# First four token tiles transposed on TensorE, all weight and cache loads moved to one DMA queue, and the MLP's place in the schedule shifted

## The chip, the cores and the metric

The kernel runs on one core of a Trainium2 chip. The core has TensorE (PE, matrix products into PSUM), VectorE (DVE), ScalarE (ACT), GpSimd (POOL) and SyncE (SP, which here only issues DMAs), and 16 DMA engines that move data between HBM and the on-chip memory (SBUF). DMAs can be issued from the queues of SP, ACT and POOL. Each engine runs its own instructions in order and waits for others by semaphores. The metric is the device time of one launch in microseconds, lower is better.

## The reference

The input `x` has 2048 tokens of 512 channels. It is layer-normalised once; the result goes through an attention block against a cache of 32 heads with 2048 keys each, and through an MLP whose first half shifts four quarters of its channels by one or two tokens. The two results are combined with `x`.

```python
xn = layernorm(x)                                  # 2048 x 512
q = (xn @ wq) as 32 heads of 128
p = softmax(q @ k_cache^T * 128 ** -0.5)           # per head 2048 x 2048
s = concat_heads(p @ v_cache) @ wo                 # 2048 x 512
h = gelu(xn @ w1)                                  # 2048 x 512
hs = token_shift(h by +1, -1, +2, -2 per quarter) @ w2
x1 = xn + hs
g = silu(x1 + gelu(layernorm(x1) @ w3) @ w4)       # w3: 512 x 1792, w4: 1792 x 512
return x + s * g
```

All data are bfloat16 in HBM; products accumulate in float32.

## The kernel before

**Tiling.** Tokens are cut into 16 tiles of 128 (NT) and 4 query blocks of 512 (QT). Heads come in 8 groups of four (HG, NG). One *unit* is one head against one query block of 512 tokens; there are 128 units, ordered by group, then query block, then head (line 113). A unit has 8 *slots* (SPU); in each slot TensorE makes the scores of 256 keys (`s_slot`, two 128x512 products into PSUM tile `ps_s`) and ScalarE turns them into exponentials `pT` (line 168). The product with V (`pv_slot`, tile `ps_o`) follows five slots later (LAG).

**What else a slot carries** is decided by hand in the loop of lines 516 to 576, by the slot number p within the unit. Slots 0 and 1: the query product of the next unit (`q_mm`, PSUM tag "xa", one buffer). Slot 0: the last additions for the softmax sum of the unit before (`add_last`, three DVE instructions). Slot 2: DVE copies the query out of PSUM (`q_copy`, line 155), and scales the output of the unit before the last (`norm`, line 218). Slot 3: `sums` (four small products, again PSUM tag "xa", then a reciprocal, then a DMA of it to HBM, line 206). Slot 4: `bcast`, the DMA that reads it back to all partitions (tile `rb`, line 210). Slots 4 and 5: the output projection of one finished token tile (`wo_mm`, also tag "xa"), read out by DVE in slot 6 (`wo_post`). Slots 2, 3 and 6, 7: half a *chunk* of the MLP each.

**The MLP.** 136 chunks are spread evenly over *windows* of half a unit, from window W0 to W1 (lines 488 and 566). First come 16 chunks of xn @ w1 (`m1_chunk`), then 16 chunks of the shifted product with w2 (`m2_chunk`), each followed by `x1` (one DVE instruction that reads PSUM tile `ps_m`) one slot later and `stats` (two DVE instructions, lines 363 and 364, and two on GpSimd) two slots later, then alternating w3 and w4 chunks. Work that belongs some slots later is put down with `at(n, fn)` and runs at the end of slot n.

**The layer norm.** `ln1_stats` loads a token tile and takes mean and variance on DVE; `rsqrt` makes 1/sqrt(var + eps) with two small GpSimd instructions; `ln1_apply` normalises on DVE (line 272), transposes the tile by a DMA on SP's queue into `xnT` (line 275), and stores it to HBM for the MLP (line 276). The first four tiles are done before the loop, the other twelve one per four slots, from slot 1 on (lines 510 to 513).

**Order and queues.** `pin` (line 61) holds an instruction in program order on its engine; what is not pinned a scheduler places. All matmuls, all DVE and ACT compute and all DMAs on SP's queue are pinned; the DMAs and the compute on POOL's queue mostly are not. On SP's queue: loads of K, transposed on the way, in four pieces of 128 KB per head (line 128), the transposes of xn, the two small softmax-sum DMAs of each unit, and the stores of the result. On POOL's queue: V (512 KB per head, line 134), wq (line 139), wo (line 143), w1 and w2 (lines 328, 329), w3 and w4, and the token tiles. The K, V, wq and wo of the next group are loaded during the last query block of a group, one head per unit (lines 520 to 529). Before the loop all four heads of the first group are loaded, and w1, w2 and wo:

```python
    for t in range(4):
        ln1_apply(t)
    for h in range(1, HG):
        load_w(h)
        load_k(h, range(KSPLIT))
        load_v(h)
    ph1_load()
    ...
    q_mm(0, range(DC))
    q_copy(0)
```

Of the kernel before, what the change touches and what calls it, by code (L numbers as in the profile page):

```python
# [17 lines left out]
def kernel(  # L18
# [15 lines left out]
    nc = tc.nc  # L34
# [42 lines left out]
    nc.vector.memset(nhalf[:], -0.5)  # L77

# [4 lines left out]
    qtp = ent(pool("qt", 2))  # L83
# [24 lines left out]
    def rsqrt(out, var):  # L108
        ve = smp.tile([P, 1], FP32, name="ve")
        nc.gpsimd.tensor_scalar(out=ve[:], in0=var, scalar1=EPS, scalar2=None, op0=ALU.add)  # L110
        nc.gpsimd.tensor_tensor(out=out, in0=ve[:], in1=nhalf[:], op=ALU.pow)
# [9 lines left out]


# [9 lines left out]
    def load_v(h):  # L132
        vBs[h] = vp.tile([P, KC, Dh], BF16, name="vb")
        nc.gpsimd.dma_start(  # L134
            out=vBs[h][:], in_=A_v_cache[0, h].rearrange("(kc p) d -> p kc d", p=P))

    def load_w(h):
        wqs[h] = wqp.tile([P, DC, Dh], BF16, name="wq_h")
        nc.gpsimd.dma_start(out=wqs[h][:], in_=wq_v[:, :, h * Dh:(h + 1) * Dh])  # L139

    def load_wo(h):
        wos[h] = wop.tile([P, D], BF16, name="wo_h")
        nc.gpsimd.dma_start(out=wos[h][:], in_=A_wo[h * Dh:(h + 1) * Dh, :])
# [89 lines left out]
    def fin_load(t):  # L233
        xl = tokp.tile([P, D], BF16, tag="ta", name="xl")
        nc.gpsimd.dma_start(out=xl[:], in_=xsrc[t])
        gl = tokp.tile([P, D], BF16, tag="ta", name="gl")
        nc.gpsimd.dma_start(out=gl[:], in_=g_d[t][:])
        fin[t] = (xl, gl)
# [19 lines left out]
    def ln1_stats(t, eng):  # L258
        xin = tokp.tile([P, D], BF16, tag="ta", name="xin")
        eng.dma_start(out=xin[:], in_=xsrc[t])  # L260
        bn = smp.tile([P, nc.vector.BN_STATS_DIM], FP32, name="bn")
        mv = smp.tile([P, nc.vector.BN_AGGR_DIM], FP32, name="mv")
        rs = smp.tile([P, 1], FP32, name="rs")
        pin(nc.vector.bn_stats(out=bn[:], in_=xin[:]))
        pin(nc.vector.bn_aggr(out=mv[:], in_=bn[:]))
        rsqrt(rs[:], mv[:, 1:2])
        ln[t] = (xin, mv, rs)

    def ln1_apply(t):
        xin, mv, rs = ln.pop(t)  # L270
        xn = tokp.tile([P, D], BF16, tag="tb", name="xn")
        pin(nc.vector.tensor_scalar(
            out=xn[:], in0=xin[:], scalar1=mv[:, 0:1], scalar2=rs[:],
            op0=ALU.subtract, op1=ALU.mult))
        pin(nc.sync.dma_start_transpose(out=xnT[:, :, t * P:(t + 1) * P], in_=xn[:]))
        nc.gpsimd.dma_start(out=xn_d[t][:], in_=xn[:])
# [50 lines left out]
    def ph1_load():  # L327
        nc.gpsimd.dma_start(out=w1_sb[:], in_=B_w1.rearrange("(dc p) j -> p dc j", p=P))
        nc.gpsimd.dma_start(out=w2_sb[:], in_=B_w2.rearrange("(jc p) c -> p jc c", p=P))
        for jc in range(DC):  # L330
            b = BASE_J[jc]
            nc.gpsimd.memset(hT[:, jc, 0:b], 0.0)
            nc.gpsimd.memset(hT[:, jc, b + Sq: Sq + PADW], 0.0)
# [9 lines left out]

    def m2_chunk(t):
        def run(i, n):
            if i == 0:
                mlp["ps"] = psX.tile([P, 512], FP32, tag="xm", name="ps_m")
                mlp["xr"] = tokp.tile([P, D], BF16, tag="tb", name="xr")
                nc.gpsimd.dma_start(out=mlp["xr"][:], in_=xn_d[t][:])
# [3 lines left out]
            if i == 1:  # L353
# [13 lines left out]
                at(n + 1, x1)  # L367
                at(n + 2, stats)
# [11 lines left out]
    def ln2(c, n):  # L380
        def start():
            mlp["xn2T"] = mp.tile([P, DC, 512], BF16, name="xn2T")
            xs = []
            for ts in range(4):
                xr = tokp.tile([P, D], BF16, tag="ta", name="x1r")
# [14 lines left out]
        for ts in range(4):  # L400
            at(n + 8 + 2 * ts, lambda ts=ts: apply(ts))
# [22 lines left out]
    def w3_prefetch():  # L424
        if w3_order:
            c, fc = w3_order.popleft()
            w = mp.tile([P, DC, 2 * P], BF16, tag="w3", bufs=3, name="w3_sb")
            nc.gpsimd.dma_start(out=w[:], in_=w3_v[:, :, fc * P:(fc + 2) * P])  # L428
# [4 lines left out]
    def m4_chunk(t, part):  # L433
# [3 lines left out]
        def run(i, n):  # L437
            if part == 0 and i == 0:
                mlp["ps"] = psX.tile([P, 512], FP32, tag="xm", name="ps_m")
                mlp["xr"] = tokp.tile([P, D], BF16, tag="tb", name="xr")  # L440
# [5 lines left out]
            if part == 2 and i == 1:  # L446
# [15 lines left out]
                at(n + 1, x2)  # L462
                at(n + 3, tanh)
                at(n + 5, silu)
# [4 lines left out]
    for tt in range(QT):  # L469
        for jc in range(DC):  # L470
            chunks.append(m1_chunk(tt, jc))
    for t in range(NT):
# [15 lines left out]
    W0, W1 = 4, 2 * (NU - 8)  # L488
# [4 lines left out]
    ln1_engs = [nc.sync, nc.scalar, nc.sync, nc.scalar]  # L493
    for t in range(4):
        ln1_stats(t, ln1_engs[t])
    load_w(0)
    load_k(0, range(KSPLIT))
    load_v(0)
    for t in range(4):
        ln1_apply(t)  # L500
    for h in range(1, HG):
        load_w(h)
        load_k(h, range(KSPLIT))
        load_v(h)
    ph1_load()
    for h in range(HG):
        load_wo(h)
    q_mm(0, range(DC))
    q_copy(0)
    for k, t in enumerate(range(4, NT)):  # L510
        n0 = 1 + 4 * k
        at(n0, lambda t=t: ln1_stats(t, nc.gpsimd))
        at(n0 + 4, lambda t=t: ln1_apply(t))

    wo_todo = deque()
    for n in range(NS + 3 * SPU):
        u, p = divmod(n, SPU)
        if u < NU:
            g, qt, hh = units[u]
            if g + 1 < NG and qt == QT - 1:  # L520
                h = (g + 1) * HG + hh
                if p == 5:
                    load_k(h, (0, 1))
                elif p == 6:
                    load_v(h)
                    load_w(h)
                elif p == 7:
                    load_k(h, (2, 3))
                    load_wo(h)
# [4 lines left out]
        if p in (0, 1) and u + 1 < NU:  # L534
# [3 lines left out]
        if p == 2 and u + 1 < NU:  # L538
# [75 lines left out]
```

## Time and profile before

| | us |
|---|---|
| median of three timed runs | 1324.67 (1320.32 to 1326.06) |
| the profiled execution, its own time | 1323.47 |
| its span, first to last instruction | 1321.7 |
| TensorE busy | 1270.7 (96%) |
| ScalarE busy | 1112.5 (84%) |
| VectorE busy | 1024.5 (78%) |
| GpSimd busy | 220.2 (17%) |
| start of the first matmul | 20.71 |
| start of the first score product | 23.36 |
| first score product of unit 4 | 68.34 |

The table is read as follows. TensorE is the engine with the most work, and a matmul of 512 columns is followed by the next after about 0.215 us at the full clock, though its own record is longer (0.38 us) because matmuls overlap in the array. What TensorE does not spend busy is 51 us. Times in the trace count from the span's start; the profiled execution's own time is 1.8 us longer than its span.

### The profile page before, as it was taken

How to read it: one execution, taken by the hardware profiler on the slowest of the kernel's cores; microseconds unless marked ns; L12 is line 12 of the kernel's file. 1: busy time of each engine (PE TensorE's matmuls, PEld its weight loads, DVE VectorE, ACT ScalarE, POOL GpSimd, SP SyncE). 2: the span in 40 equal slices, each digit the busy share in tenths (PEclk: the TensorE clock that was granted, in tenths of full speed). 3: DMA queues.
4: the chain of work that ended last, by engine and by line, in shares of the span. 5: the costliest groups of instructions: out<-in, count | busy, mean ns of one | idle time of the engine just before them, and what ended most of it. 6: DMA issues, size and time to landing. Idle time of an engine off the chain costs nothing.

```text
span 1321.7 us, 17163 instructions
## 1 busy us (share of the span) xinstructions
PE 1270.7 (96%) x6208; PEld 575.4 (44%) x6208; DVE 1024.5 (78%) x1402; ACT 1112.5 (84%) x1185; POOL 220.2 (17%) x356
## 2 busy tenths in 40 slices
PE   3899999999999999999999999999999999999995
PEld 1344444444444444444444444444444444444442
DVE  1898788888787877788877777888777888777886
ACT  2799988778999988899988889998888999888882
POOL 6630122333211021100111011001010100000101
PEclk9899999999999999999999999999999999999997
DMA  9741373234823267222652127423292312712223
GB/s 217 189 102 27 53 140 84 72 85 112 151 57 70 55 116 124 61 41 44 127 114 60 48 49 121 96 56 65 62 146 57 64 33 48 132 29 52 81 67 88
DMA packets 144468, 112.29 MB, mean 85 GB/s; under 512 B 112320, under 2 KB 114880, under 8 KB 144384
## 3 DMA queue, kind: packets, MB, share of 16 engines
q1 hardware_dynamic: 126496, 57.19, 25.0%
q0 software_dynamic: 17600, 53.76, 15.8%
q8 instruction: 48, 0.79, 0.3%
q14 instruction: 36, 0.29, 0.1%
q10 hardware_dynamic: 288, 0.26, 0.1%
HBM read 81.53 MB, written 8.65 MB: 68 GB/s over the span
## 4 chain that ended last, share of the span: by engine, by line
PE 79%; DVE 9%; ACT 6%; DMA 3%; issue 2%; POOL 1%; DVEq 0%; POOLq 0%; SPq 0%
PE ps_s L106 29%; PE ps_o L106 27%; PE ps_m L106 8%; PE ps_wo L106 8%; PE ps_q L106 6%; ACT pT L168 4%; DVE acc L179 3%; PE ps_sum L106 1%; DVE acc L184 1%; DVE qT L155 1%; ACT sq L286 1%; DMA rb<-dr 1%; DMA xin<-in_A_x_dram 1%; ACT pre L316 1%; DVE gl L250 1%
## 5 line engine op out<-in xcount | busy, mean ns | idle before, releaser
L168 ACT ACTIVATE pT<-ps_s 128x1024 bf16<-128x1024 f32 x1024 | 1015.8, 1029 | 183.0 <-PE ps_s L106 179.0
L106 PE MATMUL ps_s<-qT,kT 128*128 128x512 bf16 x2048 | 611.2, 380 | 5.0 <-DVE qT L155 2.7
L106 PE MATMUL ps_o<-pT,vb 128*128 128x512 bf16 x2048 | 610.0, 380 | 0.0
L179 DVE TENSOR_TENSOR acc<-acc,pT 128x2048 bf16<-128x2048 bf16 x256 | 312.5, 1221 | 75.2 <-ACT pT L168 70.0
L106 PEld LDWEIGHTS <-vb 128*128 128x128 bf16 x2048 | 200.0, 98 | 243.0 <-issue 1.9
L106 PEld LDWEIGHTS <-kT 128*128 128x128 bf16 x2048 | 196.4, 98 | 244.2 <-issue 26.8
L174 DVE TENSOR_TENSOR acc<-pT 128x2048 bf16<-128x2048 bf16 x128 | 156.0, 1219 | 30.9 <-ACT pT L168 30.8
L106 PE MATMUL ps_q<-xnT,wq_h 128*128 128x512 bf16 x512 | 153.9, 383 | 20.7 <-DMA xnT<-xn 20.7
L106 PE MATMUL ps_wo<-wo_h,oT 128*128 128x512 bf16 x512 | 155.2, 387 | 7.4 <-DVE s_acc L246 3.1
L246 DVE TENSOR_TENSOR s_acc<-ps_wo,s_acc 128x512 f32<-128x512 f32 x112 | 77.3, 690 | 97.9 <-PE ps_wo L106 97.9
L155 DVE CAST qT<-ps_q 128x512 bf16<-128x512 f32 x128 | 87.3, 682 | 12.3 <-PE ps_q L106 12.3
L184 DVE TENSOR_TENSOR acc<-acc 128x1024 bf16<-128x1024 bf16 x128 | 88.6, 692 | 4.4
L218 DVE TENSOR_TENSOR oT<-ps_o,rb 128x512 bf16<-128x512 f32 x128 | 87.2, 681 | 4.6 <-DMA rb<-dr 4.5
L106 PEld LDWEIGHTS <-wq_h 128*128 128x128 bf16 x512 | 50.3, 98 | 81.9 <-DMA wq_h<-in_A_wq_dram 20.7
L106 PEld LDWEIGHTS <-oT 128*128 128x128 bf16 x512 | 50.6, 99 | 73.4 <-issue 14.5
L106 PE MATMUL ps_m<-xn2T,w_sb 128*128 128x512 bf16 x224 | 66.5, 378 | 0.0
L428 POOL DMA_DIRECT2D w_sb<-in_B_w_dram x28 | 21.2, 757 | 264.0 <-PE ps_m L106 235.1
L106 PE MATMUL ps_m<-w_sb,h2T 128*128 128x512 bf16 x224 | 63.9, 379 | 0.0
L139 POOL DMA_DIRECT2D wq_h<-in_A_wq_dram x32 | 24.5, 767 | 219.7 <-PE ps_q L106 217.1
L185 DVE TENSOR_TENSOR acc<-acc 128x512 bf16<-128x512 bf16 x128 | 54.4, 425 | 4.4
L106 PEld LDWEIGHTS <-acc 128*128 128x128 bf16 x512 | 37.2, 116 | 45.7 <-issue 14.7
L134 POOL DMA_DIRECT2D vb<-in_A_v_cache_dram x32 | 37.4, 1167 | 114.9 <-PE ps_o L106 104.6
(51 smaller groups left out, 607.1 us busy)
## 6 DMA issues: line engine op xcount, KB each, us to landing
rb<-dr SPq DMA_DIRECT2D x128, 256.0 KB, 4.1
vb<-in_A_v_cache_dram POOLq DMA_DIRECT2D x32, 512.0 KB, 7.1
w_sb<-in_B_w_dram POOLq DMA_DIRECT2D x28, 256.0 KB, 4.4
wq_h<-in_A_wq_dram POOLq DMA_DIRECT2D x32, 128.0 KB, 3.1
wo_h<-in_A_wo_dram POOLq DMA_DIRECT2D x32, 128.0 KB, 4.3
kT<-in_A_k_cache_dram SPq DMA_TRANSPOSE x128, 4.8
xn_d<-xn POOLq DMA_DIRECT2D x16, 128.0 KB, 3.9
dr<-rc SPq DMA_DIRECT2D x128, 2.0 KB, 1.5
```

The source lines that it names most:

```text
L106: pin(nc.tensor.matmul(out=out, lhsT=lhsT, rhs=rhs, start=start, stop=stop))
L134: nc.gpsimd.dma_start(out=vBs[h][:], in_=A_v_cache[0, h].rearrange("(kc p) d -> p kc d", p=P))
L139: nc.gpsimd.dma_start(out=wqs[h][:], in_=wq_v[:, :, h * Dh:(h + 1) * Dh])
L155: pin(nc.vector.tensor_copy(out=qT[:], in_=st[u].pop("psq")[:]))
L168: pin(nc.scalar.activation(out=s["pT"][-1][:, jj:jj + 2, :], in_=sps[:], func=ACT.Exp, scale=SCALE))
L174: pin(nc.vector.tensor_tensor(out=s["acc"][:], in0=s["pT"][0][:], in1=s["pT"][1][:], op=ALU.add))
L179: pin(nc.vector.tensor_tensor(out=a[:], in0=a[:], in1=st[u]["pT"][i][:], op=ALU.add))
L184: pin(nc.vector.tensor_tensor(out=a[:, 0:2, :], in0=a[:, 0:2, :], in1=a[:, 2:4, :], op=ALU.add))
L185: pin(nc.vector.tensor_tensor(out=a[:, 0, :], in0=a[:, 0, :], in1=a[:, 1, :], op=ALU.add))
L218: pin(nc.vector.tensor_tensor(out=oTs[(g, qt)][:, hh, :], in0=s["o"][:], in1=s["rb"][:], op=ALU.mult))
L246: pin(nc.vector.tensor_tensor(out=sa, in0=ps[:], in1=sa, op=ALU.add))
L428: nc.gpsimd.dma_start(out=w[:], in_=w3_v[:, :, fc * P:(fc + 2) * P])
```

## The change

1. **The first four tiles.** `first_tokens` replaces the transposes by DMA for tiles 0 to 3. Each normalised tile is transposed by four products of 128 columns with an identity matrix (`ident`, made by an iota on GpSimd and a comparison on VectorE), into a buffer of `ps_o`; ScalarE copies it out into `xnT`. The query product of unit 0 is made in pieces of 128 tokens, between the transposes (`q_part`). The queries of units 1 to 3 are made in slots 0, 2 and 4 of unit 0, and copied in slots 1, 3 and 5 (the pool `qt` has four buffers instead of two).
2. **The loads.** V (in two halves of 256 KB), wq, wo, w1 and w2 go from POOL's queue to SP's, pinned; the first four wq go on ACT's queue. Heads 0 and 1 are loaded before the loop; the pieces of heads 2 and 3, w1, wo and w2 are issued at given slots from slot 2 to slot 64. Later groups: one or two pieces per unit at slots 5, 6 and 7, spread over units b-5 to b+6, where b is the first unit of a group's last query block.
3. **The other twelve tiles.** Tiles 4 to 7 are loaded at once and normalised in slots 4, 6, 13 and 15; tiles 8 to 15 take one tile per eight slots (statistics in slot 23 + 8k, normalisation and DMA transpose in slot 29 + 8k).
4. **The MLP** starts at window 10 instead of 4 (sixth unit instead of third) and ends where it did.
5. **VectorE's slots.** `evict` moves `x1` and `x2` of a chunk that ends in slot 7 into that slot instead of the next unit's slot 0. `soft` moves `stats`, the second layer norm's normalisation and `silu` to slots 3, 5 or 7.
6. **Buffers and pins.** The token tiles' pools have eight buffers per tag instead of four, the load of xn for the MLP is made one chunk ahead, and more of POOL's instructions are pinned.

```diff
+    ident = const.tile([P, P], BF16, name="ident")
+    diag = const.tile([P, P], FP32, name="diag")
+    pin(nc.gpsimd.iota(diag[:], pattern=[[-1, P]], base=0, channel_multiplier=1,
+                       allow_small_or_imprecise_dtypes=True))
+    pin(nc.vector.tensor_scalar(
+        out=ident[:], in0=diag[:], scalar1=0.0, scalar2=None, op0=ALU.is_equal))
...
-    qtp = ent(pool("qt", 2))
+    qtp = ent(pool("qt", 4))
...
-        nc.gpsimd.tensor_scalar(out=ve[:], in0=var, scalar1=EPS, scalar2=None, op0=ALU.add)
-        nc.gpsimd.tensor_tensor(out=out, in0=ve[:], in1=nhalf[:], op=ALU.pow)
+        pin(nc.gpsimd.tensor_scalar(out=ve[:], in0=var, scalar1=EPS, scalar2=None, op0=ALU.add))
+        pin(nc.gpsimd.tensor_tensor(out=out, in0=ve[:], in1=nhalf[:], op=ALU.pow))
...
+    def soft(n):
+        while n % SPU not in (3, 5, 7):
+            n += 1
+        return n
+
+    def evict(n):
+        return n if n % SPU == SPU - 1 else n + 1
...
-    def load_v(h):
-        vBs[h] = vp.tile([P, KC, Dh], BF16, name="vb")
-        nc.gpsimd.dma_start(
-            out=vBs[h][:], in_=A_v_cache[0, h].rearrange("(kc p) d -> p kc d", p=P))
+    def load_v(h, halves):
+        v = A_v_cache[0, h].rearrange("(kc p) d -> p kc d", p=P)
+        for i in halves:
+            if i == 0:
+                vBs[h] = vp.tile([P, KC, Dh], BF16, name="vb")
+            ks = slice(i * KC // 2, (i + 1) * KC // 2)
+            pin(nc.sync.dma_start(out=vBs[h][:, ks, :], in_=v[:, ks, :]))
...
+    def first_tokens():
+        xns = [ln1_norm(t) for t in range(4)]
+        st[0] = dict(psq=psX.tile([P, 512], FP32, tag="xa", name="ps_q"))
+        psq = st[0]["psq"]
+        for t in range(4):
+            tp = psO.tile([P, DC, P], FP32, tag="ps_o", name="ps_o")
+            for dc in range(DC):
+                mm(tp[:, dc, :], xns[t][:, dc * P:(dc + 1) * P], ident[:], True, True)
+            ts = slice(t * P, (t + 1) * P)
+            pin(nc.scalar.activation(out=xnT[:, :, ts], in_=tp[:], func=ACT.Identity))
+            if t >= 1:
+                q_part(t - 1, psq)
+        q_part(3, psq)
+        qT = qtp.tile([P, 512], BF16, name="qT")
+        pin(nc.vector.tensor_copy(out=qT[:, 0:3 * P], in_=psq[:, 0:3 * P]))
+        pin(nc.vector.tensor_copy(out=qT[:, 3 * P:], in_=psq[:, 3 * P:]))
...
+    def q_part(t, psq):
+        ts = slice(t * P, (t + 1) * P)
+        for dc in range(DC):
+            mm(psq[:, ts], wqs[0][:, dc, :], xnT[:, dc, ts], dc == 0, dc == DC - 1)
...
-                at(n + 1, x1)
-                at(n + 2, stats)
+                at(evict(n), x1)
+                at(soft(n + 2), stats)
...
-    W0, W1 = 4, 2 * (NU - 8)
+    W0, W1 = 10, 2 * (NU - 8)
...
+    for t, eng in enumerate([nc.sync, nc.scalar, nc.sync, nc.scalar]):
+        ln1_load(t, eng)
+    for h in range(HG):
+        load_w(h, nc.scalar)
+    load_k(0, range(KSPLIT))
+    load_v(0, (0, 1))
+    load_k(1, range(KSPLIT))
     for t in range(4):
...
+        ln1_stats(t)
+    for t in range(4, 8):
+        ln1_load(t, nc.gpsimd)
+    first_tokens()
+    load_v(1, (0, 1))
+    for t in range(4, NT):
+        stats, apply = ((2, 4), (4, 6), (10, 13), (13, 15))[t - 4] if t < 8 else (23 + 8 * (t - 8), 29 + 8 * (t - 8))
+        if t >= 8:
+            at(stats - 8, lambda t=t: ln1_load(t, nc.gpsimd))
+        at(stats, lambda t=t: ln1_stats(t))
+        at(apply, lambda t=t: ln1_apply(t))
+    for h, slots, halves in ((2, (2, 5, 6, 7), (8, 13)), (3, (14, 16, 21, 24), (22, 23))):
+        for i, n in enumerate(slots):
+            at(n, lambda h=h, i=i: load_k(h, (i,)))
+        for i, n in enumerate(halves):
+            at(n, lambda h=h, i=i: load_v(h, (i,)))
+    at(28, ph1_load)
+    at(64, w2_load)
     for h in range(HG):
...
+        at(31 + h, lambda h=h: load_wo(h))
+    for g in range(NG - 1):
+        b = (g * QT + QT - 1) * HG
+        for hh in range(HG):
+            h = (g + 1) * HG + hh
+            for i in range(KSPLIT):
+                at((b - 2 + (2 * hh + i // 2 + (hh > 0))) * SPU + (5, 7)[i % 2], lambda h=h, i=i: load_k(h, (i,)))
+            for i in range(2):
+                at((b - 2 + (2 * hh + i + (hh > 0))) * SPU + 6, lambda h=h, i=i: load_v(h, (i,)))
+            at((b + (-3, -3, 0, 0)[hh]) * SPU + (5, 7)[hh % 2], lambda h=h: load_w(h))
+            at((b - 4 - hh // 2) * SPU + (5, 7)[hh % 2], lambda h=h: load_wo(h))
...
-            if g + 1 < NG and qt == QT - 1:
-                h = (g + 1) * HG + hh
-                if p == 5:
-                    load_k(h, (0, 1))
-                elif p == 6:
-                    load_v(h)
-                    load_w(h)
-                elif p == 7:
-                    load_k(h, (2, 3))
-                    load_wo(h)
...
+        if u == 0 and p in (0, 2, 4):
+            q_mm(1 + p // 2, range(DC))
+        if u == 0 and p in (1, 3, 5):
+            q_copy(1 + p // 2)
+        if p in (0, 1) and HG - 1 <= u < NU - 1:
             q_mm(u + 1, (2 * p, 2 * p + 1))
```

## The prediction

> **What bounds the kernel now.** I read the page's busy table first, then a table of stretches, to see where TensorE is not full.
>
> ```profile
> PE 1270.7 (96%) x6208; PEld 575.4 (44%) x6208; DVE 1024.5 (78%) x1402; ACT 1112.5 (84%) x1185; POOL 220.2 (17%) x356
> PE   3899999999999999999999999999999999999995
> ```
>
> ```profile
> 0.00:20.00 20.00, 0.00 (x0) 0.00 (x0) 4.89 (x14) 1.28 (x1) 15.55 (x36) 1.00 1.01 184
> 20.00:40.00 20.00, 14.64 (x50) 5.38 (x50) 7.12 (x11) 11.53 (x12) 10.63 (x17) 1.00 1.13 253
> 40.00:60.00 20.00, 17.29 (x74) 7.42 (x75) 15.16 (x27) 13.34 (x15) 13.06 (x23) 0.83 0.80 208
> ...
> 400.00:600.00 200.00, 199.86 (x988) 91.22 (x986) 153.81 (x204) 174.84 (x188) 24.00 (x36) 1.00 0.39 76
> ```
>
> The second pair of columns is TensorE's busy time and its matmuls; the last three are granted clock, DMA share and GB/s. From 400 to 1200 us TensorE is idle for less than 1 us in all, so nothing can be won there, only lost. The idle time is at the start (20.7 us before the first matmul, 5.4 more by 40 us, 2.7 more by 60) while the DMA engines are full, in 180 to 340 us (5 us), and at the end (12 us in the last 22). Next, what TensorE waited for:
>
> ```profile
> PE ps_q L106 <- DMA xnT<-xn: 20.7, 1, 20.7
> PE ps_sum L106 <- DVE qT L155: 9.7, 15, 3.6
> ...
> PE ps_wo L106 <- DVE rc L204: 1.7, 2, 1.1
> ```
>
> Then the start in order of time, engine by engine (start, duration, engine; the bracket is the idle time before and what ended it):
>
> ```profile
> 3.39 0.69 DVE L264 BATCH_NORM_STATS2 bn<-xin 128x6 f32<-128x512 bf16 x1 [2.50 <-DMA xin<-in_A_x_dram]
> 7.76 2.13 POOL L111 TENSOR_TENSOR rs<-ve,nhalf 128x1 f32<-128x1 f32 x4
> 8.82 5.45 SPq L275 DMA_TRANSPOSE xnT<-xn  x4
> 14.33 25.41 SPq L128 DMA_TRANSPOSE kT<-in_A_k_cache_dram  x12
> 20.71 1.86 PE L106 MATMUL ps_q<-xnT,wq_h 128*128 128x512 bf16 x4 [20.71 <-DMA xnT<-xn]
> 32.90 0.69 DVE L264 BATCH_NORM_STATS2 bn<-xin 128x6 f32<-128x512 bf16 x1 [9.60 <-DMA xin<-in_A_x_dram]
> 34.54 0.59 PE L106 MATMUL ps_s<-qT,kT 128*128 128x512 bf16 x2 [1.88 <-DVE qT L155]
> 42.61 0.27 PE L106 MATMUL ps_sum<-ones_t,acc 128*128 128x1 bf16 x4 [3.60 <-DVE qT L155]
> ```
>
> The normalised tiles exist at 10.3 us, but their DMA transposes sit behind K on SP's queue and in full DMA engines until 20.7. Later a token tile that lands late (32.90) holds DVE, DVE holds `q_copy`, and that holds TensorE: 1.88 and 3.60 us. At 20.71 and after 42.61 the 512-column matmuls start 0.43 us apart instead of 0.215, for about 6 and 5 us: the clock is low after a pause. The same kind of DVE wait returns at 190 us:
>
> ```profile
> 190.35 0.68 DVE L357 SCALAR_TENSOR_TENSOR xr<-ps_m,xr 128x512 bf16<-128x512 f32 x1
> 191.07 0.69 DVE L363 BATCH_NORM_STATS2 bn<-xr 128x6 f32<-128x512 bf16 x1
> 191.80 0.18 DVE L364 BATCH_NORM_AGGREGATE mv<-bn 128x2 f32<-128x6 f32 x1
> 191.90 0.66 DVE L155 CAST qT<-ps_q 128x512 bf16<-128x512 f32 x1
> ```
>
> `x1` and `stats` stand ahead of `q_copy`; the sums need the PSUM buffer that `q_copy` empties, and TensorE idles 0.69 us, then 0.67 on the reciprocal.
>
> **The change part by part.** The sum goes against the profiled execution, 1323.47 us (1.2 below the median of the timed runs, inside their range of 1320.32 to 1326.06).
>
> *First scores.* Statistics of the four tiles are over at 6.7, as before. GpSimd now alternates `ve` (0.21) and `rs` (2.13/4 = 0.53) as each tile's statistics come, without the 0.82 us DMA issue between them: last `rs` at about 7.5. DVE normalises from 6.7 on (0.33 apart), the last tile until 8.0. The iota and the comparison come earlier; DVE waits for them ahead of the statistics, which start at 3.39. No row shows an iota; the nearest on GpSimd are 0.10 (memset) and 0.53 (pow), of one column. It begins near 0.9, so it may take 2.4 us before it costs anything; I take 0, worst case 3. ScalarE: two x and four wq issues; the last wq waits until the first K piece has landed (semaphore order), issue 1.65 plus the 4.9 to 6.0 us of these rows, so 6.6 to 7.7, then 0.45 for the issue and 1.28 for the table load: first copy at about 8.7. The chain then is copy, query piece, transposes, copy: a 128x512 copy is 0.60 (`pre<-ps_m`), four 128-column products at the low clock take between 4 x 0.107 (a quarter of the 0.427 spacing of 512 columns) and 4 x 0.427; the one-column `ps_sum` products are 0.035 apart, so cost follows columns, and I take 0.5 per four. Copies end 9.3, 9.9, 11.05, 12.05 (PSUM has two buffers), the last query piece 12.6, the two query copies (0.69 per 512 columns, so 0.75 with the split) 13.5. First score at 13.5 instead of 23.36.
>
> *Units 0 to 3.* Unit 0 took 9.3 us before, its stall left out (23.36 to 34.54, less 1.88). It now carries 12 query products instead of 4 at a low clock, beside exponentials; I take 9.5, so unit 1 starts at 23.0. Units 1 and 2 have 32 products and no query: 6.9 us of TensorE against 8 x 0.935 = 7.5 of ScalarE (six exponentials in 5.61); unit 3 has 36, 7.9. With 1 us of loss unit 4 starts at 47.0, where it started at 68.34. By then three MLP chunks had been done before (12 x 0.215 = 2.6 us) and none will be. Gain: 68.34 - 47.0 - 2.6 = 18.7.
>
> *Is K there?* SP issues a transpose in 1.27 us (5.17 for 4). Its order for heads 2 and 3 mixes K pieces with four xn transposes, V halves and, per unit, the small DMA that waits for DVE and the one that waits for it to land (1.5 to 4.6 us). Added up in that order: the first tile's xn transpose goes at about 21.6, when DVE has done slot 4; K of head 2 is issued by 28, head 3's four pieces end at 34.4, 37, 40.6 and 43. Landing takes 4.9 to 7.1, so head 2 is in time (from 31 on) and head 3, needed from 38.5 to 44.5, late by 1 to 4 us. V halves are priced between 0.32 (`rb`) and 1.27 (transpose) and count 0.5. I take -2.5, bounds 0 and -8.
>
> The Trainium skill, page "DMA: Bandwidth & Descriptors", section "Issuing engines are not separate DMA queues", says that spreading issues over engines only saves sequencer time, usually small beside the DMA. By that the move to SP's queue would cost nothing and the sum would be 2.5 us better; the issue row of 1.27 us, more than a quarter of a landing, speaks against it here.
>
> *Tiles 8 to 15.* Spread out, they unload DVE: the 0.86 us stall at 73 us goes (+0.9). But tiles 11 and 15 are normalised in slot 53 and 85, and units 8 and 12 want them in slots 56 and 88. In quiet rows an xn transpose lands 2.7 to 4.9 us after issue (median 4.0), and SP is held by `rb` first; three slots are 3.3 to 3.9 us. I take -0.5 for each, -1.0 (0 to -3).
>
> *MLP products on DVE.* In 60 to 1200 us the waits of `ps_sum` on `q_copy` are 4.4 us and of `ps_wo` on the reciprocal 1.7; less the 0.86 above, 5.2. `stats` now follows the reciprocal instead of standing ahead of `q_copy`, and `x1` falls where DVE waits for ScalarE. What is late next is `add_first`, which waits for exponentials anyway. I take +4.0, bounds 0 and 5.2.
>
> *The rest.* V, wq and wo leave POOL's queue (1.17, 0.77 and 0.54 us an issue); POOL is 17% busy and off the chain, so 0. On SP's queue later groups add 16 issues per group, 5 to 20 us in nine units; SP waits 697 us on the reciprocal, which covers them. Twenty-eight more matmuls lie in the start. w1 goes in slot 28 for slot 42, w2 in 64 for slot 150: 0. Starting the MLP later packs 136 chunks in 230 windows instead of 236, still at most one each: 0. End: the last `gl` waited 1.23 us for its load, for want of buffers, but the last addition waits for TensorE: +0.3.
>
> Sum: 18.7 - 2.5 - 1.0 + 0.9 + 4.0 + 0.3 = 20.4, so 1323.5 - 20.4 = 1303.1.
>
> The clock: page "TensorE: Matmul & The Clock Gate", Part 1, says the array runs at half clock until a window of about 3.4 us was busy. If the gaps between transposes and copies kept it cold through unit 0, units' 34 products at 0.43 would need 14.6 us instead of 9.5, and the sum would be 5 us worse; the row at 20.71, equally gappy, was warm after some 6 us.
>
> **The rivals.**
> *A, the start feeds slower (faster, by less).* K went at 25.41/12 = 2.1 us a piece before, with the DMA engines full, and landings up to 15.6 us occur. With that pace for heads 1 to 3 the last piece lands near 49.5 instead of 44.5: 5 us lost instead of 2.5, and 128-column products or an iota nearer their upper bounds take 4 more, and the DVE gain may be half: 1311. For it: the DMA share of 1.01 and 1.13. Against: w1, w2, wo and w3, over 2.2 MB, leave the first 40 us.
>
> *B, slower: `rb` behind the loads on SP's queue.* K, V and weights stand in one queue with `rb` in 9 of 16 units, seven groups, 63 units. `rb` is issued in slot 4 and needed six slots later, some 7.5 us; it lands after 4.1 (up to 7.7). If bursts of 0.5 MB make it miss by 0.5 us each time, TensorE loses 31 us: 1334. It decides from 20.4/63 = 0.32 us a unit. Against: `rb` goes ahead of the pieces in each unit, and DVE waited for it only three times (4.5 us) with K already on this queue.
>
> *C, no change.* The time saved early is lost again at one place, such as late tiles or DVE's new order stalling the MLP phase by 0.3 us in each of some 60 units: 1321.
>
> **How the numbers follow.** Main case 0.68, own range 1299 to 1308; A 0.20 (1308 to 1317); B 0.08; C 0.04. What a measurement of this kernel can tell from no change is about 0.5%, 6.6 us: faster means below 1318. Faster: main and A, 0.88; same 0.04; slower 0.08. The range 1298 to 1315 takes the main case and most of A.
>
> **What would show it.** First matmul near 7.5 us, first score 12.5 to 15; unit 4's first score at 45 to 51; no wait of `ps_sum` on `q_copy` over 0.3 us after 60 us; waits on `kT` in unit 3 of a few us; two short waits on `xnT` near 70 and 110 us. I am wrong if the iota ends after 3.4 us, if V or K waits appear in units 0 to 2, or if the table of stretches shows more than 2 us idle between 400 and 1200 us, with DVE waiting on `rb`.

## The result, and the profile after

The changed kernel takes 1307.85 us (median of six runs, 1305.01 to 1309.68) against 1323.45 us of the kernel before, run with it (six runs, 1320.32 to 1326.06): a ratio of 0.9882, with a 95% interval of 0.9859 to 0.9904, or 15.6 us less. The profiled execution of the changed kernel took 1309.66 us with a span of 1307.5, which is 13.8 us less than the profiled execution before; the steps below are counted against those two. The prediction was 1303.1 us, range 1298 to 1315.

The busy table and TensorE's row of the slices, after:

```profile
PE 1269.4 (97%) x6236; PEld 578.1 (44%) x6236; DVE 1024.6 (78%) x1404; ACT 1114.7 (85%) x1189; POOL 146.8 (11%) x259
PE   7798999999999999999999999999999999999995
```

The same stretches as before (span, TensorE busy and count, weight loads, DVE, ACT, POOL; then granted clock, DMA share, GB/s):

```profile
0.00:20.00 20.00, 10.30 (x54) 5.91 (x55) 8.03 (x22) 7.74 (x10) 8.81 (x23) 1.00 1.06 215
20.00:40.00 20.00, 17.10 (x84) 7.19 (x83) 15.52 (x26) 16.96 (x19) 7.31 (x11) 1.00 0.60 125
40.00:60.00 20.00, 15.38 (x70) 6.62 (x69) 12.53 (x20) 12.95 (x14) 5.00 (x15) 0.91 0.77 134
...
100.00:140.00 40.00, 36.45 (x169) 15.82 (x167) 30.47 (x42) 33.31 (x37) 10.73 (x16) 0.96 0.44 100
...
400.00:600.00 200.00, 199.88 (x993) 91.65 (x993) 154.94 (x206) 175.93 (x188) 13.48 (x23) 1.00 0.39 79
```

The first 40 us now hold 27.4 us of TensorE work where they held 14.6. But from 40 to 60 us TensorE is busy for *less* time than before (15.38 against 17.29), and the clock is below one between 40 and 60 and again between 100 and 140 us. What TensorE waited for:

```profile
PE ps_o L112 <- DVE xn L292: 7.2, 1, 7.2
PE ps_s L112 <- DMA kT<-in_A_k_cache_dram: 4.6, 1, 4.6
...
PE ps_q L112 <- DVE acc L201: 2.7, 1, 2.7
PE ps_o L112 <- DVE oT L234: 1.7, 1, 1.7
PE ps_sum L112 <- DVE qT L171: 1.6, 8, 0.3
...
PE ps_q L112 <- DMA xnT<-xn: 1.0, 1, 1.0
```

The wait of the first matmul went from 20.7 to 7.2 us. The waits of `ps_sum` on `q_copy` went from 9.7 us (longest 3.6) to 1.6 (longest 0.3). New are a 4.6 us wait on K, and two on token tiles: the one of 1.0 is named so; the one labelled 2.7 on `acc` is the other, as the rows below show. The start, engine by engine:

```profile
0.84 0.24 POOL L80 IOTA diag<- 128x128 f32 x1 [0.40 <-POOLq L667]
7.16 1.03 PE L112 MATMUL ps_o<-ident,xn 128*128 128x128 bf16 x8 [7.16 <-DVE xn L292]
13.31 1.01 PE L112 MATMUL ps_s<-qT,kT 128*128 128x512 bf16 x2 [0.85 <-DVE qT L317]
35.21 0.29 PE L112 MATMUL ps_sum<-ones_t,acc 128*128 128x1 bf16 x4 [1.22 <-DVE acc L201]
38.49 0.59 PE L112 MATMUL ps_o<-pT,vb 128*128 128x512 bf16 x2 [1.67 <-DVE oT L234]
50.02 0.61 PE L112 MATMUL ps_s<-qT,kT 128*128 128x512 bf16 x2 [4.57 <-DMA kT<-in_A_k_cache_dram]
51.03 1.06 PE L112 MATMUL ps_s<-qT,kT 128*128 128x512 bf16 x2
55.17 0.59 PE L112 MATMUL ps_s<-qT,kT 128*128 128x512 bf16 x2
```

The first score is at 13.31 us instead of 23.36, unit 1 starts at 22.75, and then the gain shrinks: unit 4 starts at 55.17 (68.34 before), not at 47.0. A pair of 512-column matmuls takes 0.59 us at the full clock; the rows of 1.06 from 51 us on are the lower clock that follows the pause. Two token tiles are late:

```profile
85.57 0.60 PE L112 MATMUL ps_q<-xnT,wq_h 128*128 128x512 bf16 x2 [1.03 <-DMA xnT<-xn]
129.56 1.01 PE L112 MATMUL ps_q<-xnT,wq_h 128*128 128x512 bf16 x2 [2.72 <-DVE acc L201]
```

The second stands under `acc`, which only comes last by the profile's reckoning. `acc` is finished every unit; what is different here is the transpose of tile 15, issued at 123.32 and landed 6.1 us later, at 129.47.

A useful ruler for the rest is the *lead*: the start of a unit's four small sum products (`ps_sum`) in the kernel before, less the same in the other kernel. (The sums of a unit stand in slot 3 of the next one, so the late tile of unit 12, wanted at the start of unit 11, shows in the sums of unit 10.) For the changed kernel it is 16.1 us at unit 0, 18.6 at unit 1, 14.2 at unit 3, 12.9 at unit 9, 7.7 at unit 10, 14.3 at unit 31, and from there flat to 14.0 at unit 127. So 4.4 us are lost in units 2 and 3, 5.2 at one blow between units 9 and 10, and 6.6 are won back between units 14 and 31.

### The profile page after: what moved, and what is told of

Its sections match the earlier page's. It is cut to its first block, busy times and chain, and to the rows that moved or that the text cites. A ratio compares the mean times of both kernels' runs of the same rounds, so it can differ in the third digit from the quotient of the medians.

```text
span 1307.5 us, 17205 instructions
## 1 busy us (share of the span) xinstructions
PE 1269.4 (97%) x6236; PEld 578.1 (44%) x6236; DVE 1024.6 (78%) x1404; ACT 1114.7 (85%) x1189; POOL 146.8 (11%) x259
## 4 chain that ended last, share of the span: by engine, by line
PE 83%; DVE 7%; ACT 5%; DMA 3%; issue 1%; POOL 0%; SPq 0%; ACTq 0%; DVEq 0%; POOLq 0%
PE ps_s L112 30%; PE ps_o L112 28%; PE ps_m L112 9%; PE ps_wo L112 9%; PE ps_q L112 7%; ACT pT L184 4%; DVE acc L195 3%; DMA rb<-dr 1%; PE ps_sum L112 1%; ACT sq L336 1%; DMA kT<-in_A_k_cache_dram 1%; DMA dr<-rc 1%; DVE s_acc L262 1%; DVE acc L200 1%; ACT pre L366 1%
## 5 line engine op out<-in xcount | busy, mean ns | idle before, releaser
L112 PE MATMUL ps_q<-xnT,wq_h 128*128 128x512 bf16 (+1 forms) x524 | 154.6, 380 | 5.2 <-DVE acc L201 2.7
L220 DVE RECIPROCAL rc<-ps_sum 128x4 f32<-128x4 f32 x128 | 22.9, 179 | 37.2 <-PE ps_sum L112 36.3
L517 POOL DMA_DIRECT2D g_d<-xr x16 | 8.8, 548 | 350.4 <-DVE xr L515 350.4
```

The lines of the kernel that those rows point to most:

```text
L112: pin(nc.tensor.matmul(out=out, lhsT=lhsT, rhs=rhs, start=start, stop=stop))
L220: pin(nc.vector.reciprocal(out=rc[:], in_=ps[:]))
```

## The experiments

Every edit is made to the changed kernel unless the text says otherwise. The kernel before was run along with each of the four groups of kernels; its medians there were 1322.2 to 1323.4 us, so a difference of 1 us between groups means nothing. The changed kernel itself was not run again with them; each experiment is set against its median of 1307.85 us (1305.01 to 1309.68), and the four groups ran on four different chips.

**1. Two tiles earlier (e1_tiles).** Tiles 11 and 15 are normalised and transposed six slots earlier, nine slots ahead of their use instead of three; their statistics are taken four slots earlier.

```diff
-    stats, apply = ... else (23 + 8 * (t - 8), 29 + 8 * (t - 8))
+    stats, apply = ... else (43, 47) if t == 11 else (75, 79) if t == 15 else (23 + 8 * (t - 8), 29 + 8 * (t - 8))
```

> Of the changed kernel only tiles 11 and 15 are taken earlier: statistics in slots 43 and 75 instead of 47 and 79, normalisation and DMA transpose in slots 47 and 79 instead of 53 and 85, nine slots ahead of their use instead of three. Theory (the transposed tile lands too late): the gaps ahead of the query products of units 8 and 12 (1.2 us at 85 us, 2.9 us at 127 us and half clock after it) go, the lead over the kernel before no longer falls by 5.2 us at unit 11, and the time is 5 to 6 us under that of the changed kernel, about 1302. Rival (the trace's label is right, TensorE waits for the softmax sums on DVE): the 2.7 us stay, at most 1.2 us are won, about 1306.

Measured 1302.0 us (ratio 0.9841, 0.9826 to 0.9855): 5.9 us less than the changed kernel. All that TensorE waited for between 60 and 1200 us:

```profile
PE ps_wo L112 <- DVE rc L220: 1.3, 2, 1.0
PE ps_sum L112 <- DVE qT L171: 0.3, 1, 0.3
```

With the wait on `xnT` the one labelled `acc` is gone too, although nothing about `acc` was changed: it was the tile. The lead falls by 1.0 us between units 9 and 10 instead of 5.2, so the tile's own part of that drop is 4.2 us.

**2. K around the small DMAs (e2_kgap).** K of heads 2 and 3 is issued in pairs, head 3's pairs directly after the DMA that writes the softmax sums out, in the time in which SP waits for that DMA to land.

```diff
-    for h, slots, halves in ((2, (2, 5, 6, 7), (8, 13)), (3, (14, 16, 21, 24), (22, 23))):
+    for h, slots, halves in ((2, (2, 3, 3, 3), (6, 8)), (3, (11, 11, 19, 19), (16, 22))):
```

> Of the changed kernel only the order of the loads of heads 2 and 3 on SP's queue is changed, the bytes are the same: K of head 2 in slots 2, 3, 3, 3 (ahead of the first tile transpose), V in 6 and 8; K of head 3 two pieces in slot 11 and two in slot 19, where SP otherwise only waits for the small softmax-sum DMA to land, V in 16 and 22. Theory (K was late because it stood on SP's queue behind that wait): the waits of unit 3 (4.6 us on K, 1.7 on the scaled output, 1.2 on the sums, then half clock) shrink to under 2 us, unit 4 starts near 48 us instead of 55.2, the time is 5 to 8 us lower, about 1301. Rival (the DMA engines can't bring K sooner): unit 4 starts within 2 us of 55, since the same bytes have to come.

Measured 1303.57 us (0.9849, 0.9835 to 0.9864): 4.3 us less, somewhat under the 5 to 8 that were expected; unit 4 starts at 48.46 us, as expected. SP's queue in the changed kernel (start, duration, line):

```profile
29.96 0.52 SPq L222 DMA_DIRECT2D dr<-rc  x1
33.82 0.34 SPq L226 DMA_DIRECT2D rb<-dr  x1
...
40.61 0.52 SPq L222 DMA_DIRECT2D dr<-rc  x1
43.59 0.32 SPq L226 DMA_DIRECT2D rb<-dr  x1
43.95 1.12 SPq L141 DMA_TRANSPOSE kT<-in_A_k_cache_dram  x1
...
46.37 3.60 SPq L141 DMA_TRANSPOSE kT<-in_A_k_cache_dram  x1
```

and in this version:

```profile
28.24 0.34 SPq L222 DMA_DIRECT2D dr<-rc  x1
28.63 2.95 SPq L141 DMA_TRANSPOSE kT<-in_A_k_cache_dram  x2
33.29 0.34 SPq L226 DMA_DIRECT2D rb<-dr  x1
...
37.86 0.32 SPq L222 DMA_DIRECT2D dr<-rc  x1
38.23 2.45 SPq L141 DMA_TRANSPOSE kT<-in_A_k_cache_dram  x2
41.09 0.55 SPq L226 DMA_DIRECT2D rb<-dr  x1
```

Between writing the sums and reading them back SP stands still for 2.5 to 3.3 us, and in the changed kernel head 3's third and fourth piece wait behind that. With K in this hole the read-backs go at 33.3 and 41.1 us, not later than the 33.8 and 43.6 of the changed kernel, K is all issued by 40.7 us instead of 50.0, the 4.57 us wait and the low clock behind it are gone, and the lead at unit 3 is 20.9 instead of 14.2. The drop at unit 10 is as large as it was (19.1 to 13.5).

**3. Both (e3_both).** The two edits together.

> Both edits together. If the two losses are separate: 10 to 14 us under the changed kernel, about 1296. If what one edit wins is lost again at the next late transfer: no better than the better of the two, 1301 or more.

Measured 1297.69 us (0.9809, 0.9793 to 0.9825). This is 10.2 us less than the changed kernel, the sum of 5.9 and 4.3: two separate losses, neither hidden behind the other. The version beats both kernels.

**4. VectorE's slots undone (e4_slots).** The products of the MLP and their statistics fall in the slots of the kernel before.

```diff
     def soft(n):
-        while n % SPU not in (3, 5, 7):
-            n += 1
         return n
...
-        return n if n % SPU == SPU - 1 else n + 1
+        return n + 1
```

> The changed kernel with VectorE's slots put back as before (evict is always one slot later, soft changes nothing). Theory: the short waits of the sums on the query copy in 180 to 340 us come back, 4 to 5.2 us, and the time is about 1312.5. Rival (the waits went because the start has changed, not by the slots): no change, 1308.

Measured 1312.11 us (0.9917, 0.9902 to 0.9932): 4.3 us more. Waits of TensorE between 60 and 1200 us, in the changed kernel and then here:

```profile
PE ps_sum L112 <- DVE qT L171: 0.6, 2, 0.3
```

```profile
PE ps_sum L112 <- DVE qT L169: 3.4, 7, 0.8
```

The old waits are back. TensorE's idle time from 140 to 400 us, where the w2 part of the MLP runs, was 5.55 us before, is 0.33 in the changed kernel and 3.34 here.

**5. The first tiles by DMA again (e5_dmat).** The order of loads and the queues are those of the changed kernel, but `first_tokens` is gone.

```diff
     load_k(0, range(KSPLIT))
-    load_v(0, (0, 1))
-    load_k(1, range(KSPLIT))
...
-    first_tokens()
+    for t in range(4):
+        ln1_apply(t)
+    load_v(0, (0, 1))
+    load_k(1, range(KSPLIT))
+    q_mm(0, range(DC))
+    q_copy(0)
```

> The first four tiles are transposed by DMA on SP's queue again, issued between the K pieces of head 0 and its V; everything else is as in the changed kernel. Theory (TensorE's transposes and the lighter queue share the gain at the start): the issues run from 6.8 to about 12 us, the last lands 4 to 6 us later, the first score follows 2.65 us after it as before, so near 19.5 us, 6 us later than with TensorE's transposes and 4 us earlier than in the kernel before; 1314 us (1312 to 1316). Rival (the order and the lighter queues bring it all): first score before 15.5, 1308 to 1310. Rival (only TensorE's transposes bring it): first score at 22 or later, 1317 or more.

Measured 1317.55 us (0.9963, 0.9948 to 0.9978).

```profile
17.54 1.87 PE L112 MATMUL ps_q<-xnT,wq_h 128*128 128x512 bf16 x4 [17.54 <-DMA xnT<-xn]
20.18 1.01 PE L112 MATMUL ps_s<-qT,kT 128*128 128x512 bf16 x2 [0.78 <-DVE qT L171]
...
137.62 1.01 PE L112 MATMUL ps_q<-xnT,wq_h 128*128 128x512 bf16 x2 [5.13 <-DMA xnT<-xn]
```

The first score is at 20.18 us. So of the 10.05 us that it moved, TensorE's transposes bring 6.9 and the other edits (order of loads, queues) 3.2. The total is 3.5 us worse than expected and would fit the rival that only the transposes bring it, but the first score does not. Most of the excess lies outside the start: tile 15 is later still in this execution (5.13 us of waiting at unit 12), and the lead falls by 7.6 us there instead of 5.2. Every version that leaves tile 15 in its slot pays for it, by an amount that changes with what else happens.

**6. V, wq and wo on POOL's queue (e6_pool).** For heads 4 to 31 only.

```diff
-    pin(nc.sync.dma_start(out=vBs[h][:, ks, :], in_=v[:, ks, :]))
+    pin((nc.gpsimd if h >= HG else nc.sync).dma_start(out=vBs[h][:, ks, :], in_=v[:, ks, :]))
```

(and the same for wq and wo)

> V, wq and wo of heads 4 to 31 go back on POOL's queue, at the same slots; K stays on SP's. Theory (moving them was free in the steady state): same time within 1 us of the changed kernel, 1307 to 1309, and TensorE idle less than 1 us between 400 and 1200 us; at most the transpose of tile 15 lands earlier than 6.1 us after its issue, for 1 us. Rival (the one queue holds up the small softmax-sum DMAs): 3 us or more faster. Rival (POOL's queue disturbs POOL's own work): slower by 2 us or more.

Measured 1314.41 us (0.9937, 0.9916 to 0.9958): 6.6 us more, where I had expected no difference. The profiled execution, at 1317.64 us one of the longer ones, is 8.0 us over that of the changed kernel. Its lead falls by 7.6 us between units 9 and 10 (5.2 in the changed kernel; tile 15 landed after 7.0 us), and by 5.4 between units 80 and 90:

```profile
861.23 1.03 PE L112 MATMUL ps_o<-pT,vb 128*128 128x512 bf16 x2 [3.21 <-DMA vb<-in_A_v_cache_dram]
```

```profile
856.60 0.76 POOL L485 DMA_DIRECT2D w_sb<-in_B_w_dram  x1 [17.81 <-PE ps_m L112]
857.35 0.89 POOL L151 DMA_DIRECT2D vb<-in_A_v_cache_dram  x1
```

POOL's queue had stood still for 17.81 us: a load of w3 (line 485) waited for its buffer, which TensorE had still to read, and the half of V behind it could not be issued before 857.35. It landed 3.8 us later, and TensorE waited 3.21 us for it. In these slots V should not stand in the same queue as the MLP's weights. The rival that one queue on SP holds up the softmax-sum DMAs has the wrong sign; the other one, that POOL's queue disturbs POOL's own work, has the right size, but what was held up was V.

**7. The MLP still later (e7_w0).** `W0` is 20 instead of 10, so the MLP begins in unit 10.

```diff
-    W0, W1 = 10, 2 * (NU - 8)
+    W0, W1 = 20, 2 * (NU - 8)
```

> The MLP starts at window 20 (unit 10) instead of 10 (unit 5), all else as in the changed kernel. Theory (the chunks left out early are only owed): the lead at unit 9 is larger by about 4 chunks or 2 to 4 us, and it is gone again by unit 118; the time is that of the changed kernel within 1.5 us. The tiles' late transposes at units 8 and 12 may cost more, since units without chunks are shorter: up to 2 us slower. Rival (an early start of the MLP loads TensorE while it is idle anyway): 3 us or more slower.

Measured 1310.06 us (1303.56 to 1312.07; 0.9890, 0.9858 to 0.9921): not to be told from the changed kernel. The lead at unit 9 is 17.2 instead of 12.9 us, 4.4 us more. Some five missing chunks of 0.86 us make that (nine windows at 136 chunks in 230), though 0.7 us of it was there at unit 4 already. It is 11.6 at unit 127 instead of 14.0. Chunks left out early are owed, as the prediction charged them.

**8. VectorE relieved in units 1 and 2 (e8_rs), on top of experiment 3.** Tiles 6 and 7 are normalised one and two slots later after their statistics.

```diff
-    ((2, 4), (4, 6), (10, 13), (13, 15))[t - 4]
+    ((2, 4), (4, 6), (10, 14), (13, 17))[t - 4]
```

> The version with both slot lists moved (tiles 11 and 15 earlier, K of heads 2 and 3 after the small DMAs), and in addition tiles 6 and 7 normalised one and two slots later after their statistics (slots 14 and 17 instead of 13 and 15). Theory: VectorE's two waits of 0.77 us for GpSimd's rs in unit 1 and the early unit 2 go, the sums of unit 1 come 1.2 us earlier and the second rb too; 1296.5 us. Rival: the small DMAs land when they land, whatever VectorE does; the same time, 1297.7.

Measured 1297.82 us (0.9807, 0.9788 to 0.9825), the same as experiment 3. The waits of TensorE on `acc` in the first 60 us shrank from 1.2 to 0.3 us, but the two waits on the normalised output (`oT`), which hang on the read-back, stayed at 2.3 us (2.7 in experiment 3). What is left of them in units 2 and 3 is the time in which the two small DMAs land, and not VectorE.

**9 to 11. What makes the transpose of tile 15 land late.** In the changed kernel one K piece, half of V and six loads of xn (768 KB, issued together because they are not pinned) go out beside it. e9_h4late issues head 4's K and V six slots later; e10_pinxr holds the loads of xn in program order, so that two go out and not six; e11_quiet does both.

```diff
-    ... * SPU + (5, 7)[i % 2], lambda h=h, i=i: load_k(h, (i,)))
+    ... * SPU + (5, 7)[i % 2] + 6 * (h == HG), lambda h=h, i=i: load_k(h, (i,)))
-    ... * SPU + 6, lambda h=h, i=i: load_v(h, (i,)))
+    ... * SPU + 6 + 6 * (h == HG), lambda h=h, i=i: load_v(h, (i,)))
```

```diff
-    nc.gpsimd.dma_start(out=mlp["xnext"][:], in_=xn_d[t][:])
+    pin(nc.gpsimd.dma_start(out=mlp["xnext"][:], in_=xn_d[t][:]))
```

> The K pieces and V halves of head 4 are issued six slots later, so that the transpose of tile 15 has no load behind it on SP's queue for about 4 us; the six loads of xn on POOL's queue stay beside it. Theory (the transpose lands 6.1 us after its issue because K and V pieces share the DMA engines with it): it lands within 5 us, unit 12's queries start at most 1.7 us late, the lead at the sums of unit 10 falls by 3 us or less instead of 5.2; 1305 to 1306. Rival (the six loads of xn are the cause): landing 5.8 us or more, the same drop, 1308. Rival (it would be late in any case, since the slots allow 3.3 to 3.9 us and a transpose lands 4.7 us after its issue): landing near 4.7 us, a drop of 2 to 3 us.

> The loads of xn for the MLP on POOL's queue are held in program order, so that one of them instead of six is issued beside the transpose of tile 15; K and V of head 4 stay where the changed kernel has them. Theory (K and V are the cause): landing near 6 us again, the lead falls by 5 us at the sums of unit 10; 1308. Rival (the burst of six loads): landing within 5 us, a drop of 3 us or less, 1305 to 1306.

> Both: head 4 six slots later and the loads of xn held in program order, so nothing large beside the transpose of tile 15. Every theory on what delays it expects a landing of 4 to 4.7 us here. What is left of the drop at the sums of unit 10 is then the price of the slot list alone: 0.5 to 1.4 us of waiting and, if the clock falls after it, 1.5 us more; 1304 to 1306.

Measured 1306.4 us (0.9875, 0.9855 to 0.9895), 1306.0 (0.9870, 0.9848 to 0.9892) and 1308.3 (0.9884, 0.9865 to 0.9902). The tile landed 5.7 us after its issue in all three, against 6.1 in the changed kernel: taking away the loads behind it, the loads beside it or both shortens it by 0.4 us, and both of my theories on that fell. In experiment 1 the same tile landed after 4.4 us although the DMA engines were full meanwhile (DMA share 1.01 over 112.81 to 117.18 us; 0.47 over this landing in e11_quiet). The products that wait for the tile, in e9_h4late, e10_pinxr and e11_quiet:

```profile
127.50 0.59 PE L112 MATMUL ps_q<-xnT,wq_h 128*128 128x512 bf16 x2 [2.26 <-DVE acc L201]
```

```profile
127.86 0.59 PE L112 MATMUL ps_q<-xnT,wq_h 128*128 128x512 bf16 x2 [2.24 <-DVE acc L201]
```

```profile
128.23 1.01 PE L112 MATMUL ps_q<-xnT,wq_h 128*128 128x512 bf16 x2 [2.32 <-DVE acc L201]
```

The waits are 0.08 us apart, but the first two are followed by matmuls at the full clock (0.59) and the third by the low one (1.01). The lead falls by 3.25, 3.23 and 4.89 us. So the low clock after the pause costs some 1.6 us, and it accounts for the difference between these profiled executions; the medians themselves (1306.0 to 1308.3) are hardly apart.

Whether the low clock comes depends on where the pause lies. In the clock record of each trace, the granted clock falls to 0.50 only at times that are whole multiples of 3.413 us apart (in the changed kernel at 50.74, 129.24 and 1293.19 us, which is 23 and 341 steps), and outside the last 25 us it stays there for one or two such steps. Cut into windows along this grid, the pauses look like this (idle time is the window less TensorE's busy time in it):

| run, pause of TensorE (us) | idle time in each window that holds it | granted clock in the window after |
|---|---|---|
| e10_pinxr, 2.24 | 1.26, 0.97 | 1.00, 1.00 |
| e9_h4late, 2.26 | 1.10, 1.16 | 1.00, 1.00 |
| e7_w0 at unit 8, 1.99 | 2.04 | 0.50 |
| e11_quiet, 2.32 | 2.13 (the other 0.19 in the next) | 0.50 |
| changed kernel at unit 12, 2.72 | 2.40 (the other 0.32 in the next) | 0.50 |
| changed kernel in unit 3, 4.57 | 1.88, 2.69 | 1.00, 0.50 |

A pause of 1.99 us within one window brought the low clock, and one of 2.26 us cut in two by the grid did not: the length of the pause alone does not decide. In the fourteen profiled executions, from 30 us on, every full-clock window with 2.03 us or more of idle time (37 windows) was followed by the low clock, and no window with 1.88 us or less; none lies between. No run moved a pause along the grid on purpose; this is read from the traces as they are.

**12. Ahead of the read-back (e12_before_rb).** Tiles 11 and 15 two slots earlier, so that the transpose goes before the broadcast `rb` on SP's queue.

```diff
-    29 + 8 * (t - 8)
+    (27 if t in (11, 15) else 29) + 8 * (t - 8)
```

> Tiles 11 and 15 are normalised two slots earlier (slots 51 and 83 instead of 53 and 85), so that their transposes stand between the two small softmax-sum DMAs on SP's queue instead of behind the second; K, V and the loads of xn stay where the changed kernel has them. Theory (the broadcast of 256 KB issued 0.4 us ahead is what makes the transpose land after 5.7 us even with nothing behind it): landing near 3.7 us, no wait on it at units 8 and 12, 1302 as with the tiles four and more slots earlier. Rival (the broadcast has no part in it): landing 5 to 6 us again; the issue is about 1.7 us earlier, so unit 8 has no wait, unit 12 waits 0.5 to 1.5 us and its clock stays full; 1303 to 1304.5.

Measured 1302.36 us (0.9841, 0.9808 to 0.9873).

```profile
118.84 0.34 SPq L222 DMA_DIRECT2D dr<-rc  x1
119.28 1.21 SPq L299 DMA_TRANSPOSE xnT<-xn  x1
120.58 0.53 SPq L226 DMA_DIRECT2D rb<-dr  x1
```

```profile
124.70 0.59 PE L112 MATMUL ps_q<-xnT,wq_h 128*128 128x512 bf16 x2 [0.50 <-issue]
```

Tile 11 landed in 3.5 us (4.7 in the changed kernel), tile 15 in 5.3. TensorE does not wait at unit 8 and waits 0.50 us at unit 12, at the full clock. The landing of tile 11 would fit the theory (3.7 us), that of tile 15 fits the rival: the broadcast ahead of it does not explain it either. (It was still issued, 1.3 us behind the transpose, with K, V and the six loads of xn; a version with none of these near the tile was not run.) By the medians the two slots alone are worth 5.5 us, nearly the 5.9 of the six slots of experiment 1, though the interval of this ratio overlaps that of the changed kernel. Why this tile takes 5.3 to 6.1 us (7.0 in e6_pool, but 4.4 in e1_tiles) and the tiles from 9 to 14 mostly 3.5 to 5.3 stays open; tile 8 takes 6.1 to 7.0 us in the changed kernel and all its versions, without harm, since it is wanted much later.

## Why the prediction was right or wrong

**The first scores: right.** 13.5 us was predicted, 13.31 measured; first matmul "near 7.5", measured 7.16. The steps between agree too: the first copy starts at 8.68 (8.7), the last query piece ends at 12.47 (12.6). The iota, for which no row stood, took 0.24 us at 0.84. Experiment 5 shows that the transposes on TensorE are the larger part of it.

**Unit 0: right.** Unit 1 was to start at 23.0 us and started at 22.75; TensorE did not stay at the low clock through unit 0 (pairs of 512-column matmuls take 0.59 us from 17.94 on), as the Trainium skill's page "TensorE: Matmul & The Clock Gate", Part 1, could be read to allow at a price of 5 us.

**"Is K there?": right in kind, wrong in size; this is one of the two steps that failed.** It took 2.5 us, with a bound of 8. Against the start of 47.0 that the prediction gave for unit 4, 8.2 us were lost. The wait on K was 4.57 us and the low clock behind it cost about 1.7: 6.3 us instead of 2.5. Waits of 1.22 on the sums and 1.67 on the scaled output make 2.9 us, where the 47.0 held 1 us of loss. The sum of the queue had head 3's four issues end at 34.4, 37, 40.6 and 43 us; they ended at 37.9, 40.5, 45.1 and 50.0. The sum did count the stops at the small DMAs, but too short: with its own issue times, its steps from 28 to 34.4 and from 37 to 40.6 leave about 2.2 and 1.7 us for them (an estimate), and they took 3.3 and 2.5. It also priced every issue of K at 1.27 us, and the last one took 3.60. The write of the sums landed after up to 3.8 us in this stretch, where 1.4 is its median over the run. What the step did not see is that these stops need not hold K at all: experiment 2 takes the loss away by order alone, 4.3 us by the medians, 6.7 us of lead at unit 3. The Trainium skill, page "DMA: Bandwidth & Descriptors", section "Issuing engines are not separate DMA queues", calls the issue time usually small beside the DMA; by that nothing should have been lost. The row of 1.27 us an issue that was set against it has the right sign, but in these rows the two stops of a queue that issues in order cost more than the ordinary issues do.

**"Tiles 8 to 15": the other step that failed.** 0.9 for the vanished stall was taken, and -0.5 for each of tiles 11 and 15. The wait at unit 8 was 1.03 us and the lead falls by that much there. At unit 12 it was 2.72 us, then 1.6 at the low clock; the lead falls by 5.2 us, of which 1.0 remains in experiment 1 and is not the tile's. Together -5.2 by the lead, and -5.9 by the medians of experiment 1, instead of -1.0 and outside the bound of -3. The median of 4.0 us for a landing, taken from quiet rows, was used for two transposes whose slots leave 3.3 to 3.9 us; for tiles 9 to 15 a landing took 4.1 to 6.1 us, and no price was put on the clock.

**"MLP products on DVE": right.** +4.0 was predicted; undoing it costs 4.3 us (experiment 4), and idle time from 140 to 400 us falls by 5.2.

**The end: right.** From the last pair of scores to the end it was 25.6 us and is 25.4; +0.3 was predicted.

**The debt of the MLP: right in kind.** The 2.6 us were charged; experiment 7 shows that missing chunks are paid back, spread over the whole run.

**The queues: right for the changed kernel, for an incomplete reason.** POOL's and SP's queues were costed at 0 and TensorE is idle for only 0.5 us from 400 to 1200 us (0.8 before). Experiment 6 shows what the step did not see: with V in the new slots, the old queue would cost 6.6 us.

**The sum.** Of the 20.4 us, 5.7 went in units 2 and 3 (8.2 instead of 2.5) and 4.2 at the tiles (5.2 instead of 1.0); that would leave 10.5. By the two profiled executions 13.8 were won. Of the 3.3 us between, VectorE's stretch explains 1.2 (5.2 of idle time instead of 4.0); the remaining 2 us lie in small changes of the lead and are not attributed. So the total came nearer to the prediction than its two worst terms, and that part was luck. One reading of the start counts 0.7 us twice (the 5.4 us idle by 40 us hold the end of the 20.7 before the first matmul); no term rests on it.

**The rivals.** A, with a slower start, is partly what happened: its 5 us at K were 6.3, but its other parts (iota, 128-column products, half of the DVE gain) did not come. B did not happen: VectorE waited for `rb` once between 400 and 1200 us, for 0.5 us, and experiment 6, which takes V, wq and wo of heads 4 to 31 off SP's queue, is slower. C did not happen; its mechanism, late tiles, did, at a third of its price.

## What to carry to other kernels

A queue that issues in order has to be priced by its waits: list which instruction on it waits for what, and put the bulk loads into the holes behind a DMA that must land, and not behind the DMA that waits for it. A median landing time is no margin; give a transpose that an engine will wait for the longest landing of its stretch, since two slots more cost nothing here and were worth about 5 us by the medians. Short pauses of TensorE should be priced with the clock that may follow: here one pause of 2.3 us cost itself and another of 2.3 cost 1.6 us more, because nearly all of it fell into one window of the 3.413 us grid.

## What was not expected of the hardware

- The low clock came after pauses of TensorE that were short: after waits of 1.99, 2.32, 2.72, 3.21 and 5.13 us pairs of matmuls took 1.01 to 1.06 us, after 2.24 and 2.26 us 0.59, and after the wait of 4.57 us in unit 3 the low clock came one pair later. The Trainium skill, page "TensorE: Matmul & The Clock Gate", Part 1, has the clock fall after an idle window of about 3.4 us, and the window run freely. The grid of 3.413 us in the traces agrees with a window that runs freely. It does not agree with a window that has to be idle throughout: 2.03 us of idle time in 3.41 were enough in all 37 cases here, and 1.88 were not.
- The transpose of one 128x512 tile by DMA landed 3.4 to 7.0 us after its issue within the same 70 us of these kernels, 5.7 us with little beside it (DMA share 0.47 over the landing in e11_quiet) and 4.4 with full engines (1.01 in e1_tiles).
- The write of 2 KB of softmax sums takes 1.4 us in the median and 3.8 and 3.0 us at 30 and 41 us, where the DMA share is 0.60 (20 to 40 us) to 0.77 (40 to 60); on an in-order queue that alone stopped SP for 3.3 and 2.5 us.
- An iota over 128x128 on GpSimd took 0.24 us, less than a power of 128 values (0.57 to 0.61 us each for the first four tiles of the same run).
